# Order list with GpSimd's passes and the shared port, GpSimd's sums interleaved with the next products, VectorE's score blocks from the first period on

## The chip, the cores and the metric

The kernel runs on one core of one Trainium2 chip. A time is the device time of one execution in microseconds (us). The kernel before takes 893.42 us, the median of 3 runs (892.31 to 895.25).

A core has five engines, each with its own instruction queue that it works through in order: TensorE (PE, matrix products), VectorE (DVE), ScalarE (ACT, exponents), GpSimd (POOL) and SyncE (SP, which here issues all DMA transfers). Engines wait for each other on semaphores only.

## The reference

Two attention blocks over the same input x (2048 tokens, 512 features, 32 heads of 16 features), mixed by a gate for each token:

```python
def reference(A_x, A_wqkv, A_wo, B_x, B_wqkv, B_wo, gate_w):
    # _A_ref: full attention
    scores = jnp.einsum("bhqd,bhkd->bhqk", q, k) * (Dh ** -0.5)
    p = _softmax(scores, axis=-1)
    o = jnp.einsum("bhqk,bhkd->bhqd", p, v)
...
    # _B_ref: each token looks at 8 tokens: itself and 2, 4, ... 14 before it
    W, dil = 8, 2
    idx = pos[:, None] - off[None, :]
    logits = jnp.einsum("bhsd,bhswd->bhsw", q, kg) * scale
    attn = _softmax(logits, axis=-1)
    o = jnp.einsum("bhsw,bhswd->bhsd", attn, vg)
...
    x = A_x
    g = _sigmoid((x * gate_w).sum(-1, keepdims=True))
    a = _A_ref(x, A_wqkv, A_wo)
    b = _B_ref(x, B_wqkv, B_wo)
    return g * a + (1 - g) * b
```

Each block ends in a product with its own output matrix. All tensors are bfloat16.

## The kernel before

**Full attention (block A).** The work is cut into 32 *periods*: four chunks of 512 queries, and in each eight groups of four heads. A period has 64 *score blocks*, one for each of its four heads and each of 16 key tiles: 128 keys by 512 queries. For a score block TensorE multiplies keys and queries into PSUM; an exponent is taken; and TensorE multiplies the result with the values and adds it up in one PSUM bank (`acc`). The exponents go two ways:

- *On ScalarE*: score blocks are taken in sets of three and two (tile `ring`), with one ACTIVATE a set that writes `pT`. `pT` has five buffers.
- *On VectorE*: a block's scores go to a PSUM bank `D`; one TENSOR_SCALAR turns them into a 16-bit number (tile `dt_a`, or a part of `wkv` once the weights in it are used up), four such blocks side by side; then four passes over the 2048 columns (tile `pd_a`, again with spare parts) make four shifted approximations of the exponent. They are multiplied with four copies of the values that carry four weights (`vd_all`). `n_dve` says how many of a period's 64 blocks go this way: 0 in the first four periods, then 4, 8, 4, 8, then 8 and 12 in turn; 264 in all, so that ScalarE keeps 1784.

Between two periods VectorE moves `acc` out (`accT`, po1), divides by the sums (po2) and transposes (po3).

**Local attention (block B).** 16 tiles of 128 tokens (`b_tile`, line 776). For each: TensorE projects keys, values and queries, VectorE copies them out (`kvs`, `qb`), SyncE writes keys and values to a scratch in memory (`kv_scr`) and reads them back shifted by the eight offsets, in two halves of four offsets (`ksh` and `vsh`, two buffers each). GpSimd does the arithmetic, two offsets at a time:

- `logits_mul` (835): four products of 256 elements into `prod`, which has one buffer;
- `logits_add` (846): sums over the 16 features of a head by halving: two passes of 256 elements, one of 256, one of 128, and one of 64 into `lg`;
- softmax over the eight offsets: `sm_pre` on VectorE (max `mx` and subtraction), an exponent on ScalarE, `sm_post` on VectorE;
- `av_mul` (887) and `av_add` (904): four products of weights and values, then the sums into `ob` and at the end `obb`.

Then TensorE transposes `obb` (four transposes a tile, line 946 in `fin`), VectorE copies them to `obt`, and the output product (`ab_part`) adds both blocks for 128 tokens. Tile t+1's logits come ahead of tile t's weighted sums on GpSimd.

**What sets the order.** Every piece of work is an `Op` with an engine, a length that the author put in (`occ`), a due time (`dl`), what it needs (`deps`) and the buffers it takes and uses (`Tok`, `Res`). `list_schedule` (line 149) goes through time, starts on each engine the op with the earliest due time among those that can start, and returns all ops in the order of their planned starts. The instructions are then issued in that order on every engine and tied to it. So the lengths do not change the work; they decide where on each queue an instruction stands, and an engine that comes to an instruction whose input is late waits there with all that is behind it. Where the list sees TensorE idle it adds products with a zero tile (`z`) that keep it busy. GpSimd's work is entered as one op for four products (2.52 or 2.41 us) and one op for their sums (2.68, 1.37 or 2.74); when such an op meets one of VectorE's `pd_a` passes in the plan, both are stretched by fixed factors (`BESIDE`, `UNDER`). The due times of block B come from `b_start` and `b_space`: tile t is due `b_space` after tile t-1. The four scaled copies of the values (`evd`, line 669, in `v_proj`) are one op for each tile of keys, four TENSOR_SCALAR, entered with 0.43 + 0.032 us a head.

In the profile nearly all instructions of VectorE, ScalarE, GpSimd and SyncE have line 315 and those of TensorE line 324, where a helper records each one; so it is read by the names of the tiles. The line numbers given here are those of the kernel before.

Of the kernel before, what the change touches and what calls it, by code (L numbers as in the profile page):

```python
# [41 lines left out]
NPT = 5  # L42
LATE0 = 8
NDL = 3
SPREAD = (0.85, 0.9)
# [18 lines left out]
class Op:  # L64

    def __init__(self, eng, occ, fn, dl, deps=(), alloc=(), use=(), lat=None, rel=0.0, name="",
                 mode="f", js=(), full=0.0, fill=False, scores=None, after=(), ride=False):
        self.scores, self.ride = scores, ride
        self.eng, self.occ, self.fn, self.dl, self.rel, self.name = eng, occ, fn, dl, rel, name
        self.mode, self.js, self.full, self.fill, self.filled = mode, list(js), full, fill, 0  # L70
        self.after = [d for d in after if d is not None]
        self.deps, self.alloc = [d for d in deps if d is not None], list(alloc)
        if lat is None:
            lat = 0.0 if eng == "pe" else (occ(0.0) if callable(occ) else occ) + LAT[eng]
# [13 lines left out]
BESIDE, UNDER = 0.575, 0.52  # L88
# [3 lines left out]
P1D, SHD = -100.0, 2.0  # L92
# [56 lines left out]
def list_schedule(ops, zeros):  # L149
# [16 lines left out]
    def avail(o):  # L166
        t = o.ready
        for tk in o.alloc:
            r = tk.res
            n = len(r.order)  # L170
            if n >= r.cap:
                for u in r.order[n - r.cap].ops:
                    if u.done is None:
                        return INF
                    t = max(t, u.done)
# [15 lines left out]
    shift, glob = (0.0, 0.0), (0.0, 0.0)  # L191
    while len(out) < len(ops):
# [24 lines left out]
        if e == "pe":  # L217
            tz, n = arr.idle(o, t)
            if n > 0:
                z = zeros(n)  # L220
                tz = max([tz, avail(z)] + [u.t for tk in z.alloc[0].res.order[-2:] for u in tk.ops if u.done is not None and u.t < t])
                if tz + n * PASS + (0.0 if o.mode == "c" else SWITCH) <= t + 0.05:
# [3 lines left out]
                    z.done = end + LAT[e]  # L226
# [6 lines left out]
        else:  # L233
            occ, lat = o.occ, o.lat
            if e == "pool" and occ > 1.3:
                more = max(0.0, min(shift[1], t + occ / UNDER) - max(shift[0], t)) * (1.0 - UNDER)
                occ, lat, glob = occ + more, lat + more, (t, t + occ + more)
            if callable(occ):
                occ = o.occ(t)
                if glob[0] <= t < glob[1]:  # L240
                    occ /= BESIDE
                    free["pool"] += (min(t + occ, glob[1]) - t) * (1.0 - UNDER)
                lat = o.lat + occ
                shift = (t, t + occ)
            o.t, o.end, o.done = t, t + occ, t + max(occ, lat)
# [3 lines left out]
        for s_ in succ.get(o, ()):  # L249
            left[s_] -= 1  # L250
            if left[s_] == 0:
                s_.ready = max([s_.rel] + [d.end if d.eng == s_.eng else d.done for d in s_.deps] + [d.t for d in s_.after])
# [5 lines left out]
def kernel(  # L258
# [154 lines left out]
    rowc = const.tile([128, 3], FP32, name="rowc")  # L413
    z32 = const.tile([128, 32], BF16, name="z32")
# [24 lines left out]
    def init_dve():  # L439
# [8 lines left out]
        V.memset(z32[:], 0.0)  # L448

# [31 lines left out]
    def load_x(sc):  # L481
        def s():
            xl = work.tile([128, W // 2, D], BF16, name="xld", tag=("ksh", "vsh")[sc % 2], bufs=2)
# [31 lines left out]
    xtok = [tok(("ksh", "vsh")[sc % 2], 2) for sc in range(NC)]  # L515
    tw = tok("pd", NPD)
    o_x = [None] * NC
# [70 lines left out]
    def k_proj(i, sc, tag, dl, rel=0.0):  # L588
# [16 lines left out]
        return op("dve", 0.78, kc, dl, deps=[b], use=[tk])  # L605

    def k_bound(i, dl):
# [21 lines left out]
        a = op("dve", 0.3, mx, dl - 2.5, deps=o_kc[i])  # L629
        b = op("pe", 0.1, sw, dl - 2.0, full=0, deps=[a, o_perm], alloc=[tk])  # L630
        c = op("dve", 0.2, ng, dl - 1.2, deps=[b], use=[tk])
        if i == 0:
            o_k[i] = [op("dve", 0.32, fill(sc * QW, (sc + 1) * QW), dl + 0.1 * sc, deps=[c]) for sc in range(NC)]
        else:
            o_k[i] = [op("dve", 0.95, fill(0, S), dl, deps=[c])] * NC
# [14 lines left out]
    def v_proj(h0, h1, tb, TB, tag, dl, rel=0.0):  # L650
# [18 lines left out]
        def evd(t):  # L669
            def s():  # L670
                for m in range(NV):
                    V.tensor_scalar(out=vd_all[:, m, t - (NT - NTD), h0:h1, :], in0=vp_all[:, t, h0:h1, :],
                                    scalar1=WEIGHTS[m] * 2.0 ** -DEXP, scalar2=None, op0=ALU.mult)
            return s
# [7 lines left out]
        for t in range(max(tb, NT - NTD), tb + TB):  # L682
            d = op("dve", 0.43 + 0.032 * (h1 - h0), evd(t), max(dl, S0[4]) + 2.0, deps=[c])
            for h in range(h0, h1):
                o_vd[(h, t)] = d
# [12 lines left out]
    def q_proj(pi, tag, dl, rel=0.0):  # L698
# [25 lines left out]
        o_q[pi] = op("dve", 0.35, ab, dl, deps=[c], use=[tq])  # L724
# [51 lines left out]
    def b_tile(t):  # L776
# [45 lines left out]
        def load(key, off, hf):  # L822
            def s():
                r0 = 16 + t * 128 - DIL * hf * WH
                base = kv_scr[r0:r0 + 128, off * D:(off + 1) * D]
                st[key, hf] = work.tile([128, WH, D], BF16, name=key, tag=key, bufs=2)
                SP.dma_start(out=st[key, hf][:], in_=_ap(base, [[2 * D, 128], [-DIL * 2 * D, WH], [1, D]]))
            return s
        tks, tvs = [tok("ksh", 2), tok("ksh", 2)], [tok("vsh", 2), tok("vsh", 2)]
# [5 lines left out]
        def logits_mul(hf, wp):  # L835
            def s():
                if hf == 0 and wp == 0:
                    st["lg"] = work.tile([128, H, W], FP32, name="lg", tag="lg", bufs=2)
                st["prod"] = work.tile([128, WP, D], FP32, name="prod", tag="prod", bufs=1)
                for w_ in range(WP):  # L840
                    for c0 in range(0, D, HB):
                        G.tensor_tensor(out=st["prod"][:, w_, c0:c0 + HB], in0=st["ksh", hf][:, wp + w_, c0:c0 + HB],
                                        in1=st["qb"][:, c0:c0 + HB], op=ALU.mult)
            return s

        def logits_add(hf, wp):
            def s():
                lg = st["lg"]
                pv_ = st["prod"][:].rearrange("p w (h d) -> p w h d", d=DH)
                n = DH  # L850
                while n > 2:
                    n //= 2
                    ws = min(WP, max(1, HB // (H * n)))
                    for w0 in range(0, WP, ws):
                        G.tensor_tensor(out=pv_[:, w0:w0 + ws, :, 0:n], in0=pv_[:, w0:w0 + ws, :, 0:n],
                                        in1=pv_[:, w0:w0 + ws, :, n:2 * n], op=ALU.add)
# [6 lines left out]
            return s  # L863

        def sm_pre():
            lg = st["lg"]
            mx = work.tile([128, H], FP32, name="mx", tag="mx", bufs=1)
            V.tensor_reduce(out=mx[:], in_=lg[:], axis=AX.X, op=ALU.max)
            mx_bc = _ap(mx[:], [list(mx[:].ap[0]), [1, H], [0, W]])
# [5 lines left out]
        def sm_post():  # L875
# [4 lines left out]
            V.reciprocal(out=rr[:], in_=ssum[:])  # L880
            V.tensor_scalar(out=rr[:], in0=rr[:], scalar1=omg[:, t:t + 1], scalar2=None, op0=ALU.mult)
            rr_bc = _ap(rr[:], [list(rr[:].ap[0]), [1, H], [0, W]])
# [4 lines left out]
        def av_mul(hf, wp):  # L887
            def s():
                if wp == 0:
                    key = ("ob", "obb")[hf]  # L890
                    st[key] = work.tile([128, D], (FP32, BF16)[hf], name=key, tag=key, bufs=1)
                attn = st["lg"]
                st["prod"] = work.tile([128, WP, D], FP32, name="prod", tag="prod", bufs=1)
                for w_ in range(WP):
                    for c0 in range(0, D, HB):
                        w0 = hf * WH + wp + w_
                        a0 = attn[:, c0 // DH:c0 // DH + hn, w0:w0 + 1]
                        attn_bc = _ap(a0, [list(a0.ap[0]), [W, hn], [0, DH]])
                        G.tensor_tensor(out=st["prod"][:, w_, c0:c0 + HB].rearrange("p (h d) -> p h d", d=DH),
                                        in0=st["vsh", hf][:, wp + w_, c0:c0 + HB].rearrange("p (h d) -> p h d", d=DH),  # L900
                                        in1=attn_bc, op=ALU.mult)
            return s

        def av_add(hf, wp):
            def s():
                prod, ob = st["prod"], st["ob"]
                for c0 in range(0, D, HB):
                    cs = slice(c0, c0 + HB)
                    if not hf and not wp:
                        G.tensor_tensor(out=ob[:, cs], in0=prod[:, 0, cs], in1=prod[:, 1, cs], op=ALU.add)  # L910
                        continue
                    G.tensor_tensor(out=prod[:, 0, cs], in0=prod[:, 0, cs], in1=prod[:, 1, cs], op=ALU.add)
                    G.tensor_tensor(out=(st["obb"] if hf and wp else ob)[:, cs], in0=ob[:, cs], in1=prod[:, 0, cs], op=ALU.add)
            return s

        def chain_ops(fs, dls, deps, alloc, use, last_use=()):
            a = None
            for n_, (f, d, occ) in enumerate(fs):
                if n_ % 2 == 0:
                    tp = tok("prod", 1)  # L920
                a = op("pool", occ, f, dls + 0.01 * n_, deps=deps if a is None else [a],
                       alloc=(alloc if a is None else []) + ([] if n_ % 2 else [tp]),
                       use=use + (alloc if a is not None else []) + ([tp] if n_ % 2 else []), name=f"B{t}")
            return a
        lgs = [[(g(hf, wp), 0, c) for wp in range(0, WH, WP) for g, c in ((logits_mul, 2.52), (logits_add, 2.68))] for hf in range(2)]
# [358 lines left out]
```

## Time and profile before

| what | value |
|---|---|
| median of 3 runs | 893.42 us (892.31 to 895.25) |
| the profiled execution | 894.26 us |
| its span, first to last instruction | 892.1 us |
| mean clock granted to TensorE | 0.983 |
| exponents of block A on ScalarE | 714 ACTIVATE, 816.6 us |
| GpSimd's block-B passes | 1056, from 37.1 to 851.7 us |
| exponents of block A on VectorE | 264 passes `pd_a`, 963 and 960 ns; 264 passes from `D`, 681 and 682 ns |

The profile is of one execution. Each engine has its busy time; a group's row has its count, busy time and mean length, and the idle time just before its instructions with the engine that ended it. The page cuts the span into 40 slices with the busy share of each in tenths. The chain that ended last is followed back from the last instruction, each time to what released it; its shares say which engines' work set the end. An engine may have a high busy share and yet not set it, or wait seldom and set it all the same.

### The profile page before, as it was taken

What the parts mean: (1) busy time and instruction counts of PE and PEld (TensorE: products, weight loads), DVE (VectorE), ACT (ScalarE), POOL (GpSimd) and SP (SyncE); (2) the same over time, 40 slices, a digit from 0 to 9 for tenths busy, and PEclk for the clock granted to TensorE, in tenths of its full rate; (3) what the DMA queues carried; (4) which work ended last, traced back from release to release, by engine and by line L of the source; (5) the groups of instructions that cost most, each with busy time, mean ns of one, the idle gap of its engine ahead of it and who ended that gap; (6) DMA issues with size and microseconds to landing.
All of it is one profiled execution on the core that took longest, in us unless ns stands there. A gap on an engine that the chain in (4) does not pass through costs nothing.

```text
span 892.1 us, 18870 instructions
## 1 busy us (share of the span) xinstructions
PE 817.3 (92%) x7413; PEld 260.0 (29%) x7413; DVE 675.7 (76%) x1120; ACT 825.3 (93%) x736; POOL 786.4 (88%) x1088
## 2 busy tenths in 40 slices
PE   7898988987899999999999988999999999999997
PEld 3333323333232222222222222222223222222231
DVE  4344747688767988888797978888798787868866
ACT  2889999997999999999999998999999999999996
POOL 4369999999999999999999999999999999999910
PEclk9889999999999999999999999999999999999999
DMA  8310302020202111111112111011111210101000
GB/s 281 111 61 1 105 15 93 15 72 26 95 24 73 60 61 48 36 49 48 47 37 65 65 38 48 31 59 44 60 48 43 66 48 25 48 2 37 12 1 24
DMA packets 44440, 47.37 MB, mean 53 GB/s; under 512 B 2352, under 2 KB 41776, under 8 KB 44352
## 3 DMA queue, kind: packets, MB, share of 16 engines
q1 hardware_dynamic: 44352, 46.18, 16.0%
q8 instruction: 58, 0.95, 0.4%
q14 instruction: 30, 0.25, 0.1%
HBM read 39.85 MB, written 6.32 MB: 52 GB/s over the span
## 4 chain that ended last, share of the span: by engine, by line
POOL 51%; PE 16%; ACT 12%; DVE 11%; issue 8%; DMA 1%; POOLq 0%; SPq 0%; DVEq 0%; ACTq 0%
POOL prod L315 43%; ACT pT L315 12%; PE misc_ps L324 6%; PE ring L324 4%; PE acc L324 4%; POOL ob L315 4%; POOL obb L315 2%; DVE pd_a L315 2%; POOL lg L315 2%; DVE dt_a L315 1%; DVE wkv L315 1%; DVE lg L315 1%; PE D L324 1%; DVE vd_all L315 1%; DVE kt_all L315 1%
## 5 line engine op out<-in xcount | busy, mean ns | idle before, releaser
L315 ACT ACTIVATE pT<-ring 128x1536 bf16<-128x1536 f32 x714 | 816.6, 1301 | 41.2 <-PE acc L324 20.7
L324 PE MATMUL ring<-qt,kt_all 32*128 32x512 bf16 x1784 | 282.0, 386 | 29.6 <-ACT pT L315 24.3
L315 POOL TENSOR_TENSOR prod<-prod 128x256 f32<-128x256 f32 x352 | 278.9, 800 | 10.0
L315 POOL TENSOR_TENSOR prod<-ksh,qb 128x256 f32<-128x256 bf16 x256 | 184.9, 752 | 32.9 <-DMA ksh<-kv_scr 21.4
L324 PE MATMUL acc<-pT,vp_all 128*17 128x512 bf16 (+1 forms) x1784 | 194.1, 390 | 0.9 <-DVE accT L315 0.7
L315 POOL TENSOR_TENSOR prod<-vsh,lg 128x256 f32<-128x256 bf16 x256 | 182.1, 741 | 5.0
L324 PEld LDWEIGHTS <-kt_all 32*128 32x128 bf16 x2048 | 90.8, 91 | 300.8 <-issue 292.3
L324 PE MATMUL misc_ps<-z 128*32 128x512 bf16 x507 | 158.6, 385 | 2.6 <-DVE z L315 1.6
L315 DVE TENSOR_SCALAR pd_a<-wkv 128x2048 uint16<-128x2048 uint16 x160 | 150.1, 963 | 1.3
L315 DVE TENSOR_SCALAR wkv<-D 128x512 uint16<-128x512 f32 x160 | 109.0, 681 | 43.3 <-PE D L324 42.7
L324 PE MATMUL acc<-pd_a,vd_all 128*17 128x512 bf16 x1056 | 108.3, 385 | 3.9 <-DVE pd_a L315 3.0
L324 PE MATMUL D<-qt,kt_all 32*128 32x512 bf16 x264 | 100.9, 382 | 6.6 <-DVE dt_a L315 2.9
L315 DVE TENSOR_SCALAR pd_a<-dt_a 128x2048 uint16<-128x2048 uint16 x104 | 97.2, 960 | 0.8
L315 DVE TENSOR_SCALAR dt_a<-D 128x512 uint16<-128x512 f32 x104 | 70.9, 682 | 34.7 <-PE D L324 33.8
L324 PEld LDWEIGHTS <-z 128*32 128x32 bf16 x621 | 54.5, 96 | 76.1 <-issue 45.7
L324 PEld LDWEIGHTS <-vp_all 128*17 128x17 bf16 (+1 forms) x1784 | 44.7, 88 | 84.7 <-issue 78.1
L324 PE MATMUL misc_ps<-bw,xT 128*128 128x512 bf16 x192 | 56.3, 390 | 7.5 <-DVE qt L315 3.6
L315 POOL TENSOR_TENSOR ob<-ob,prod 128x256 f32<-128x256 f32 x64 | 56.1, 877 | 5.0
L315 DVE TENSOR_SCALAR_CACHE_REDUCE kt_all<-misc_ps,rowc 128x512 bf16<-128x512 f32 x32 | 23.9, 748 | 30.7 <-PE misc_ps L324 30.6
L324 PEld LDWEIGHTS <-vd_all 128*17 128x17 bf16 x1056 | 30.7, 88 | 50.3 <-issue 42.2
L324 PEld LDWEIGHTS <-xT 128*128 128x128 bf16 x576 | 30.5, 98 | 42.5 <-issue 37.0
L324 PE MATMUL misc_ps<-xT,wkv 128*32 128x512 bf16 x384 | 38.4, 389 | 3.7 <-DVE xT L315 1.9
(78 smaller groups left out, 607.5 us busy)
## 6 DMA issues: line engine op xcount, KB each, us to landing
ksh<-kv_scr SPq DMA_DIRECT2D x32, 512.0 KB, 4.0
vsh<-kv_scr SPq DMA_DIRECT2D x32, 512.0 KB, 3.7
kv_scr<-kvs SPq DMA_DIRECT2D x16, 256.0 KB, 2.0
xld<-in_A_x_dram SPq DMA_DIRECT2D x4, 512.0 KB, 6.8
out_dram<-osb SPq DMA_DIRECT2D x16, 128.0 KB, 1.7
bw<-in_B_wqkv_dram SPq DMA_DIRECT2D x1, 1536.0 KB, 10.1
wkv<-in_A_wqkv_dram SPq DMA_DIRECT2D x2, 512.0 KB, 6.9
pd_a<-in_A_wqkv_dram SPq DMA_DIRECT2D x1, 512.0 KB, 8.0
```

Source lines behind the costliest of these rows:

```text
L315: return chain_on(key, f(*a, **k))
L324: return chain(nc.tensor.matmul(out, lhsT=lhsT, rhs=rhs, start=start, stop=stop, **kw))
```

## The change

It has these parts:

1. *The list's costs.* GpSimd's work is entered pass by pass, each as 0.14 us of its own (`PRE`) and then a time per element (`NS`) in which it holds a port shared with VectorE. VectorE's 16-bit passes (`SB`) and its passes with two inputs of 64 elements or more (`TT`) hold the same port. In the plan only one holds it at a time. An op that needs another op of the same engine may start `SELF` behind its end (0.11 us on GpSimd). Several lengths are changed to match.
2. *GpSimd's order within a tile.* `prod` has two buffers. The sums of one pair of offsets are issued in turn with the products of the next pair. In the weighted sums the two halves of each step are issued next to each other.
3. *Scaled values.* `vd_all` is made by one TENSOR_TENSOR with a small tile of weights (`wts`) for a block of heads instead of four TENSOR_SCALAR for each key tile: 5 instructions instead of 60, due from the first period on.
4. *VectorE's blocks*: 4 in each of the first four periods, 8 in each of the next four, then 8, 8, 8, 12 in turn. The sum is still 264.
5. *Buffers*: keys, values and the first three loads of x share one tag `gat` with three buffers, and the key and value loads are tied to one order on SyncE's queue (keys of tile t+1, then values of tile t). `pT` becomes three buffers of three blocks and three of two.
6. *Due times*: `b_start` 36, `b_space` 44, 47 and 49; accT's eviction ahead of everything on VectorE; an output tile needs only its own tile's `obt`, not those of its whole chunk.

The core of the diff:

```diff
-    n_dve=(0,) * 4 + (4, 8) * 2 + (8, 12) * 12,
+    n_dve=(4,) * 4 + (8,) * 4 + (8, 8, 8, 12) * 6,
...
-    b_start=40.0,
-    b_space=(41.0,) * 4 + (44.5,) * 4 + (47.5,) * 8,
+    b_start=36.0,
+    b_space=(44.0,) * 4 + (47.0,) * 4 + (49.0,) * 8,
...
-NPT = 5
+NPT = 3
+NGA = 3
...
-SPREAD = (0.85, 0.9)
+SPREAD = (0.75, 0.8)
...
+SELF = dict(pe=0.0, dve=0.09, act=0.05, pool=0.11, sp=0.0)
+NS = dict(bb=0.00189, bf=0.00178, ff=0.00212)
+PRE = 0.14
+SB = lambda n: [(True, 0.065 + n / 3840.0)]
+TT = lambda n: [(n >= 64, 0.075 + n / 960.0)]
...
-            occ, lat = o.occ, o.lat
-            if e == "pool" and occ > 1.3:
...
+            occ = o.occ
+            if o.parts is not None:
+                u = t
+                for shared, p in o.parts:
+                    if shared:
+                        u = port = max(u, port) + p
+                    else:
+                        u += p
+                occ = u - t
...
-        def evd(t):
-            def s():
-                for m in range(NV):
-                    V.tensor_scalar(out=vd_all[:, m, t - (NT - NTD), h0:h1, :], in0=vp_all[:, t, h0:h1, :],
-                                    scalar1=WEIGHTS[m] * 2.0 ** -DEXP, scalar2=None, op0=ALU.mult)
...
+        def evd():
+            w = wts[:]
+            k0, n_ = t0 - (NT - NTD), (h1 - h0) * (DH + 1)
+            V.tensor_tensor(out=vd_all[:, :, k0:k0 + nt, h0:h1, :].rearrange("p m t h d -> p m t (h d)"),
+                            in0=_ap(vp_all[:, t0, h0, 0:1], [list(vp_all[:].ap[0]), [0, NV], [H * (DH + 1), nt], [1, n_]]),
+                            in1=_ap(w, [list(w.ap[0]), [1, NV], [0, nt], [0, n_]]), op=ALU.mult)
...
+        lseq = lgs[0][:nm]
+        for g_ in range(len(halves)):
+            nxt = lgs[g_ + 1][:nm] if g_ + 1 < len(halves) else []
+            ad = lgs[g_][nm:]
+            lseq += ad[:2]
+            for k_ in range(max(nm, na - 2)):
+                lseq += nxt[k_:k_ + 1] + ad[2 + k_:3 + k_]
...
+    turn = loads["k", 0]
+    for t in range(NT):
+        turn = turn + loads.get(("k", t + 1), []) + loads["v", t]
+    for o1, o2 in zip(turn, turn[1:]):
+        o2.after.append(o1)
...
-        a = op("dve", 0.64, po1, E - 1.0, deps=o_pv[pi], alloc=[ta], use=[acc_tok[pi]])
+        a = op("dve", 0.64, po1, E - PO1D, deps=o_pv[pi], alloc=[ta], use=[acc_tok[pi]])
...
-                   deps=[a] if k0 else [o_oat[NG * c_ + ng - 1], o_wo] + o_obt[TPC * c_:TPC * (c_ + 1)],
+                   deps=[a] if k0 else [o_oat[NG * c_ + ng - 1], o_wo] + o_obt[t:t + 1],
```

Here `lgs[g_]` holds the passes of one pair of offsets: `nm` = 4 products and `na` = 5 sums. So between two sums of one pair a product of the next pair is issued.

In the built programs VectorE issues the same 264 blocks, GpSimd the same passes in another order, and TensorE 443 + 120 products with the zero tile instead of 507 + 114.

More of the change, by code (lines that the diff above doesn't have):

```diff
@@ L66, in __init__ @@
     def __init__(self, eng, occ, fn, dl, deps=(), alloc=(), use=(), lat=None, rel=0.0, name="",
-                 mode="f", js=(), full=0.0, fill=False, scores=None, after=(), ride=False):
-        self.scores, self.ride = scores, ride
+                 mode="f", js=(), full=0.0, fill=False, scores=None, after=(), ride=False, parts=None):
+        self.scores, self.ride, self.parts = scores, ride, parts
+        if parts is not None:
+            occ = sum(p for _, p in parts)
         self.eng, self.occ, self.fn, self.dl, self.rel, self.name = eng, occ, fn, dl, rel, name
@@ L87 @@
 SH_LAT = 0.3
-BESIDE, UNDER = 0.575, 0.52
 GT = 32.0
@@ L174, in avail @@
                         return INF
-                    t = max(t, u.done)
+                    t = max(t, u.end + SELF[u.eng] if u.eng == o.eng else u.done)
         return t
@@ L225, in list_schedule @@
                     z.t, end = arr.put(z, tz)
-                    z.done = end + LAT[e]
+                    z.end, z.done = end, end + LAT[e]
                     extra.append(z)
@@ L251, in list_schedule @@
             if left[s_] == 0:
-                s_.ready = max([s_.rel] + [d.end if d.eng == s_.eng else d.done for d in s_.deps] + [d.t for d in s_.after])
+                s_.ready = max([s_.rel] + [d.end + SELF[d.eng] if d.eng == s_.eng else d.done for d in s_.deps] + [d.t for d in s_.after])
                 cand[s_.eng].append(s_)
@@ L448, in init_dve @@
         V.memset(z32[:], 0.0)
+        for m in range(NV):
+            V.memset(wts[:, m:m + 1], WEIGHTS[m] * 2.0 ** -DEXP)
     def init_pool():
@@ L885, in b_tile, with av_mul @@
         hn = HB // DH
-        def av_mul(hf, wp):
+        def av_mul(hf, wp, w_, c0):
             def s():
-                if wp == 0:
+                if wp == 0 and w_ == 0 and c0 == 0:
                     key = ("ob", "obb")[hf]
                     st[key] = work.tile([128, D], (FP32, BF16)[hf], name=key, tag=key, bufs=1)
+                if w_ == 0 and c0 == 0:
+                    st["prod", hf, wp] = work.tile([128, WP, D], FP32, name="prod", tag="prod", bufs=2)
                 attn = st["lg"]
[L893 to L902, printed above, removed]
@@ L904, in av_add @@
-        def av_add(hf, wp):
-            def s():
[L906 to L911, printed above, removed]
+                w0 = hf * WH + wp + w_
+                a0 = attn[:, c0 // DH:c0 // DH + hn, w0:w0 + 1]
+                attn_bc = _ap(a0, [list(a0.ap[0]), [W, hn], [0, DH]])
@@ new lines, in s, with av_add @@
+                G.tensor_tensor(out=st["prod", hf, wp][:, w_, c0:c0 + HB].rearrange("p (h d) -> p h d", d=DH),
+                                in0=st["vsh", hf][:, wp + w_, c0:c0 + HB].rearrange("p (h d) -> p h d", d=DH),
+                                in1=attn_bc, op=ALU.mult)
+            return s, "bf", HB
+        def av_add(hf, wp, c0, k_):
+            def s():
+                prod, ob = st["prod", hf, wp], st["ob"]
+                cs = slice(c0, c0 + HB)
+                if not hf and not wp:
+                    G.tensor_tensor(out=ob[:, cs], in0=prod[:, 0, cs], in1=prod[:, 1, cs], op=ALU.add)
+                elif k_ == 0:
@@ new lines, in chain_ops @@
+        def chain_ops(seq, dls, alloc, toks):
+            made, tps, a, seen = {}, {}, None, set()
+            for n_, (g_, k_, (f, kind, n), src, deps) in enumerate(seq):
+                new = g_ not in tps
+                if new:
+                    tps[g_] = tok("prod", 2)
+                al, us = list(alloc.get((g_, k_), ())), []
+                for tk_ in toks(g_):
+                    if tk_ not in al:
+                        us.append(tk_)
+                (al if new else us).append(tps[g_])
+                a = op("pool", 0.0, f, dls + 0.001 * n_, deps=deps + ([made[g_, src]] if src is not None else []),
+                       after=[a], alloc=al, use=us, name=f"B{t}", parts=[(False, PRE), (True, NS[kind] * n)])
+                made[g_, k_] = a
+            return a
@@ new lines, in b_tile @@
+        halves = [(hf, wp) for hf in range(2) for wp in range(0, WH, WP)]
+        mulp = lambda g, hf, wp: [g(hf, wp, w_, c0) for w_ in range(WP) for c0 in range(0, D, HB)]
+        adds = []
+        n_ = DH
+        while n_ > 2:
+            n_ //= 2
+            ws = min(WP, max(1, HB // (H * n_)))
+            adds += [(n_, w0, ws) for w0 in range(0, WP, ws)]
+        nm, na = WP * (D // HB), len(adds) + 1
+        lgs = []
+        for g_, (hf, wp) in enumerate(halves):
+            ps_ = mulp(logits_mul, hf, wp) + [logits_add(hf, wp, *x) for x in adds] + [logits_out(hf, wp)]
+            srcs = [None] * nm + [1, 3] + list(range(nm + 1, nm + na - 1))
+            lgs.append([(g_, k_, p_, srcs[k_], ([lk[hf], qa] if k_ == 0 else [])) for k_, p_ in enumerate(ps_)])
@@ new lines, in b_tile @@
+        a = op("dve", 0.0, sm_gate, tb + SMD, deps=[a, o_g], parts=[(True, 0.1)])
+        a = op("dve", 0.0, sm_mul, tb + SMD, deps=[a], use=[tlg], parts=TT(H * W))
+        for g_, (hf, wp) in enumerate(halves):
+            k1 = range(1 if not hf and not wp else 2)
+            ps_ = mulp(av_mul, hf, wp) + [av_add(hf, wp, c0, k_) for k_ in k1 for c0 in range(0, D, HB)]
+            srcs = [None] * nm + [2, 3] + [nm, nm + 1]
+            aseq += [(g_, k_, p_, srcs[k_], ([lv[hf], a] if k_ == 0 else [])) for k_, p_ in enumerate(ps_)]
```

136 lines of the change are left out of this document (66 added, 70 removed).

## The prediction

> **What bounds the kernel now.** I read the page's busy shares first, then the chain that ended last, then the table of windows, the waits and short pieces of the timeline. Shares and chain, from the page:
>
> ```profile
> PE 817.3 (92%) x7413; PEld 260.0 (29%) x7413; DVE 675.7 (76%) x1120; ACT 825.3 (93%) x736; POOL 786.4 (88%) x1088
> ...
> ACT  2889999997999999999999998999999999999996
> POOL 4369999999999999999999999999999999999910
> ...
> POOL 51%; PE 16%; ACT 12%; DVE 11%; issue 8%; DMA 1%; POOLq 0%; SPq 0%; DVEq 0%; ACTq 0%
> ```
>
> ScalarE (ACT) is the fullest engine, yet half of the chain that ended last is GpSimd (POOL). GpSimd is busy without a break from about 75 us to 850 us. The windows show what that does to ScalarE (columns: window, then busy us and count of PE, PEld, DVE, ACT, POOL, then TensorE's clock):
>
> ```profile
> 25.00:50.00 25.00, 23.24 (x233) 8.19 (x232) 6.94 (x26) 20.68 (x20) 12.25 (x21) 0.80 0.31 96
> 50.00:75.00 25.00, 23.41 (x289) 8.91 (x285) 13.40 (x41) 24.78 (x24) 17.35 (x29) 1.00 0.17 54
> ...
> 200.00:225.00 25.00, 20.27 (x192) 8.37 (x188) 21.13 (x39) 18.84 (x17) 23.82 (x37) 0.93 0.08 23
> ...
> 525.00:550.00 25.00, 21.28 (x175) 5.71 (x175) 18.13 (x27) 22.30 (x21) 23.90 (x35) 0.93 0.17 54
> ...
> 700.00:725.00 25.00, 22.27 (x206) 6.23 (x199) 22.40 (x33) 22.81 (x21) 24.21 (x30) 1.00 0.15 46
> ```
>
> Summed over the whole table, ScalarE stands idle 2.7 us of 150 between 50 and 200 us (1.8%), and 30.9 us of 650 between 200 and 850 us (4.8%). How GpSimd, which feeds ScalarE nothing but one small exponent a tile, can stop it shows in the waits (engine waiting, what it waited for: total us, times, longest) and in the timeline around 802 us (start, duration, engine):
>
> ```profile
> ACT pT L315 <- PE acc L324: 20.7, 16, 5.0
> ...
> PEld L946 <- POOL obb L315: 9.0, 8, 2.0
> DVE mx L315 <- POOL lg L315: 7.5, 7, 2.5
> ...
> PE misc_ps L946 <- POOL obb L315: 7.0, 5, 1.8
> ```
> ```profile
> 802.04 0.31 POOL L315 TENSOR_TENSOR lg<-prod 128x64 f32<-128x64 f32 x1
> 802.38 0.42 DVE L315 TENSOR_REDUCE mx<-lg 128x32 f32<-128x256 f32 x1 [1.49 <-POOL lg L315]
> ```
>
> TensorE and VectorE work through fixed orders. The order list puts a tile's four transposes (L946) and its softmax (mx) where it believes GpSimd will be done. In the trace, the transposes of tiles 0 to 4 start 2.6 to 4.5 us after GpSimd's obb is written, those of tiles 6 to 15 mostly 0.1 to 1.0 us after it; mx starts 0.03 us after lg in seven of the last eight tiles. So from about 400 us on GpSimd is later than the list thinks, TensorE and VectorE stand at these instructions, and all score blocks queued behind them come late. GpSimd's steady pace is (802.4 - 436.6)/7 = 52.3 us a tile between the softmaxes of tiles 8 and 15.
>
> I count score blocks (one ring matmul each, 1784 in all) in front of a tile's transposes in the built instruction order, and set them against the trace: tile 4 has 585 in front and starts at 307.3 us, tile 6 808 at 409.8, tile 8 1020 at 512.5, tile 14 1668 at 825.3, tile 15 1723 at 851.8. Pace: 0.460 us a block from tile 4 to 6, 0.483 from 8 to 14; from tile 0 (190 at 114.5) to 1 (285 at 159.1) 0.469. ScalarE's own floor is 816.6/1784 = 0.458.
>
> **The change part by part.**
>
> *GpSimd's dependent passes.* Four passes of a weighted sum, before:
>
> ```profile
> 102.94 0.73 POOL L315 TENSOR_TENSOR prod<-prod 128x256 f32<-128x256 f32 x1
> 103.75 0.72 POOL L315 TENSOR_TENSOR ob<-ob,prod 128x256 f32<-128x256 f32 x1
> 104.43 0.72 POOL L315 TENSOR_TENSOR prod<-prod 128x256 f32<-128x256 f32 x1
> 105.23 0.73 POOL L315 TENSOR_TENSOR ob<-ob,prod 128x256 f32<-128x256 f32 x1
> ```
>
> Start to start it is 0.81 and 0.80 us where a pass needs the one just before, 0.68 where it does not: 0.12 us a dependence. By the code a tile has 26 such neighbours (16 in the logits, where prod has one buffer, so the next product waits too; 10 in the weighted sums); the trace has 414 such gaps for 16 tiles. Interleaved and with two prod buffers, three a tile stay (the sums of the last pair of offsets). 23 x 0.12 = 2.8 us a tile, 44 us in all: 49.5 instead of 52.3 a tile. The other bound is nothing, if VectorE's hold on the port fills what the gaps leave. I take most of it, since a gap of 0.12 us is short beside a VectorE pass of 0.68 us or more.
>
> The Trainium skill (SBUF — State Buffer, section "SBUF: two separate sides") says that GpSimd and VectorE share a port pair as an exclusive lock for the whole instruction, for VectorE passes in a two-port mode or with two SBUF inputs. The trace agrees in that the pd_a pass takes 0.675 us at the least and 1.05 at the median, and a 256-element GpSimd pass 0.72 or about 1.17. By that rule a gap taken out is partly a gap in which VectorE got in anyway, and the saving is less than 44; its result is the second rival below.
>
> *The order list.* In the built order of the changed kernel the transposes have 203, 305, 405, 520, 625, 735 ... 1605, 1715, 1765 blocks in front (before 190, 285, 388, 480, 585, 698 ... 1560, 1668, 1723), about 110 a tile. At 0.465 us a block that is 51.2 us a tile: GpSimd at 49.5 keeps ahead. Behind tile 15's transposes 19 blocks are left instead of 61. This takes away the two L946 waits (16.0 us) and mx (7.5 us), and with them most of what held ScalarE after 200 us. Next late is ScalarE itself.
>
> *The scaled values vd_all.* Sixty TENSOR_SCALAR (13.1 + 2.3 = 15.4 us in the groups) become five TENSOR_TENSOR, two of 816 elements and three of 1632. No such pass is in the trace. From rden (16 elements, 0.18 us at 211.3 us) and lg<-lg,mx (256, 0.42 at the least) I get 1.0 ns an element: 1.0 and 1.8 us, together 7.4; at ott's mean of 646 ns for 256 elements 16.5. I take 7.4, since the uncontended row is the nearer in kind. The worth is in the place: the largest stall of the whole run is
>
> ```profile
> 205.83 2.54 DVE L315 TENSOR_SCALAR vd_all<-vp_all 128x136 bf16<-128x136 bf16 x4
> ...
> 211.54 1.02 ACT L315 ACTIVATE pT<-ring 128x1024 bf16<-128x1024 f32 x1 [5.01 <-PE acc L324]
> ```
>
> where four passes, which the old list costs at 0.69 us together, take 2.54 and make accT and the next period late. It goes, 5 us.
>
> *VectorE's blocks from the first period.* The count stays: 264 blocks, 1784 exponents' blocks. Each costs VectorE 0.68 + 0.96 = 1.65 us. The first four periods get 4 each (6.6 us in some 28, where windows show 7 to 16 of 25 busy), the next four 8 instead of 4 and 8, the late ones 9 on average instead of 10. ScalarE's sum is unchanged, so by itself this is worth 0; it evens VectorE out (22 to 23.7 of 25 in windows like 650 to 675 now). Without that cover, periods 4 to 7 are the tight ones: see the last rival.
>
> *Buffers and queue.* Three gather buffers for keys and values instead of four, loads in a forced order on SP's queue: a half tile lasts GpSimd some 12 us, and a load lands 3.4 to 6.2 us after its issue, two halves ahead; 0, and up to 1.5 us a tile (24) if loads queue behind a late store there. Six exponent buffers instead of five and accT's eviction first: these act on "ACT pT <- PE acc", 20.7 us; between 0 and that, counted within the pace below.
>
> **The sum.** Up to block 285 (159.1 us) I change nothing. The other 1499 blocks at 0.465 (between the 0.460 and 0.469 of the stretches where GpSimd did not yet press) take 697.0: 856.1. Now the 61 blocks after tile 15's transposes end with the span after 40.3 us, of which 61 x 0.483 = 29.4 is pace and 10.9 tail. 856.1 + 10.9 = 867.0 of span. The profiled execution took 894.26 for 892.1 of span (+2.2) and stands 0.8 above the median: 868.4, **869** said.
>
> **The rivals.**
> 1. *ScalarE without a stall*: pace 0.458 from block 285 on. Speaks for it that windows of 24.9 and 25.0 busy exist; against, that no long stretch keeps it. 686.5 instead of 697.0: 858.
> 2. *GpSimd binds as before* because the port eats the gaps: its end stays at 851.7, and 19 blocks at 0.483 plus 10.9 follow: 871.8 of span, 873. It decides if less than 1.1 of the 2.8 us a tile survives.
> 3. *The list is no truer than before*, stalls come back elsewhere, for each one removed: 893. For it: the chain also has PE, DVE and ACT pieces (490 to 514, 594 to 669 us); against: the misjudged costs are just those named above.
> 4. *Slower: VectorE becomes the bound in periods 1 to 7*, where projections, scaled values and the new blocks meet. Busy is 21 of 25 from 200 to 250 us now; 4 more blocks add 6.6. If each of the seven periods lost what the window 200 to 225 loses (6.2 us, 5.7 over the usual), that is 40: 909. It decides from 3.5 us a period on, where the gain is used up. Against: VectorE stood at 7 to 16 of 25 in periods 0 to 3, and 8 us of vd_all go.
>
> **How the numbers follow.** Forecast 0.58 (869), rival 1 0.12, rival 2 0.15, rival 3 0.06, rival 4 0.09. A measurement of this kernel tells about 0.3% (2.7 us) from no change: faster 0.85, same 0.06, slower 0.09. The range holds the forecast and rivals 1 and 2 (0.85): its low end is rival 1 less the 4.3 us that ScalarE loses in the window 25 to 50 us, should the first blocks on VectorE relieve it there, 854; its high end is rival 2 with half of the 24 us that queued loads could cost, 885.
>
> **What would show it.** Right: GpSimd at 49 to 50 us a tile, gaps between its passes nearly gone; the L946 waits on obb and mx on lg down from 23.5 us to a few; ScalarE idle about 2% of 200 to 850; the 5 us stall gone; the chain led by ACT or PE. Wrong: mx or the transposes still starting at once behind GpSimd (rival 2), VectorE above 24 of 25 before 260 us with "ACT pT <- PE acc" grown (rival 4), or key and value loads that GpSimd waits for.

## The result, and the profile after

The changed kernel takes 879.12 us (median of 4 runs, 878.21 to 882.45), the kernel before on the same chip 893.76: ratio 0.9843, interval 0.9812 to 0.9874. The forecast was 869; of the 24 us it promised, 14.6 came. From the page of the changed kernel (span 880.7 us):

```profile
PE 793.0 (90%) x7310; PEld 257.8 (29%) x7355; DVE 694.6 (79%) x1069; ACT 820.7 (93%) x736; POOL 781.6 (89%) x1088
...
ACT  2889996589899999999999999999999999999996
POOL 5287999379999999999999999999999999999830
...
ACT 43%; PE 22%; issue 18%; DVE 15%; DMA 1%; SPq 0%; DVEq 0%; ACTq 0%
```

GpSimd, 51% of the chain before, is no longer in it at all; ScalarE leads. But both rows have a hole in the seventh to ninth of the 40 slices that was not there before. The windows:

```profile
125.00:150.00 25.00, 16.00 (x160) 5.34 (x158) 19.76 (x20) 16.22 (x15) 24.77 (x40) 0.80 0.07 22
150.00:175.00 25.00, 14.57 (x143) 6.26 (x144) 21.48 (x24) 15.19 (x15) 11.27 (x18) 0.80 0.18 60
...
200.00:225.00 25.00, 23.32 (x263) 8.53 (x266) 23.29 (x45) 23.44 (x22) 24.77 (x35) 1.00 0.16 54
...
525.00:550.00 25.00, 23.99 (x207) 7.65 (x207) 17.47 (x26) 25.00 (x23) 24.76 (x38) 1.00 0.07 22
...
700.00:725.00 25.00, 22.69 (x194) 6.99 (x197) 20.95 (x31) 24.96 (x24) 25.00 (x34) 1.00 0.36 105
```

From 200 to 850 us ScalarE is idle 5.0 us of 650 (30.9 before): better than forecast. From 50 to 200 us it is idle 22.9 of 150 (2.7 before), 18.6 of it in the first two windows shown, where TensorE's granted clock also falls to 0.80. The waits say who was waited for there:

```profile
POOL prod L320 <- DVE qb L320: 27.9, 2, 20.0
...
ACT pT L320 <- PE ring L329: 16.9, 10, 8.6
...
PE acc L329 <- DVE pd_a L320: 11.4, 12, 8.3
ACT pT L320 <- PE D L329: 10.6, 2, 9.5
PE misc_ps L329 <- DVE vp_all L320: 10.3, 5, 9.1
```

ScalarE waits for TensorE, TensorE once for VectorE's `pd_a` (8.3 us) and once for its `vp_all` (9.1 us), and later GpSimd for VectorE's `qb`. VectorE's timeline has two instructions out of all proportion (start, duration); the second, `rden`, stands ahead of that `vp_all` in VectorE's queue:

```profile
127.08 0.68 DVE L320 CAST qt<-misc_ps 128x512 bf16<-128x512 f32 x1
127.68 8.93 DVE L320 TENSOR_SCALAR pd_a<-dt_a 128x2048 uint16<-128x2048 uint16 x1
136.52 0.21 DVE L320 SCALAR_TENSOR_TENSOR negk<-misc_ps,rowc 128x1 f32<-128x1 f32 x1
...
152.06 9.25 DVE L320 TENSOR_TENSOR rden<-rden,g_rw 128x16 f32<-128x16 f32 x1
161.34 0.42 DVE L320 TENSOR_TENSOR ott<-accT,rden 128x256 bf16<-128x256 f32 x1
```

The same pd_a pass takes 0.68 us when nothing is in its way, and `rden` has sixteen elements. In both stretches GpSimd runs pass after pass:

```profile
127.90 0.68 POOL L320 TENSOR_TENSOR prod<-ksh,qb 128x256 f32<-128x256 bf16 x1
128.53 0.73 POOL L320 TENSOR_TENSOR prod<-prod 128x256 f32<-128x256 f32 x1
129.20 0.68 POOL L320 TENSOR_TENSOR prod<-ksh,qb 128x256 f32<-128x256 bf16 x1
129.83 0.41 POOL L320 TENSOR_TENSOR prod<-prod 128x128 f32<-128x128 f32 x1
```

Each starts about 0.05 us before the one ahead ends. ScalarE, in the same stretch, with its two stalls:

```profile
138.76 16.43 ACT L320 ACTIVATE pT<-ring 128x1536 bf16<-128x1536 f32 x14 [8.59 <-PE ring L329]
164.71 1.45 ACT L320 ACTIVATE pT<-ring 128x1536 bf16<-128x1536 f32 x1 [9.52 <-PE D L329]
```

So a theory was at hand. **Theory 1 (port):** the interleaving took away the gaps by which VectorE gets the shared port; in two places it got none for 8 to 9 us. **Theory 2 (VectorE's load),** the fourth rival of the prediction: VectorE is overfull in these periods, since its blocks now start early.

### The profile page after: what moved, and what is told of

Its sections match the earlier page's. It is cut to its first block, busy times and chain, and to the rows that moved or that the text cites. A ratio compares the mean times of both kernels' runs of the same rounds, so it can differ in the third digit from the quotient of the medians.

```text
span 880.7 us, 18629 instructions
## 1 busy us (share of the span) xinstructions
PE 793.0 (90%) x7310; PEld 257.8 (29%) x7355; DVE 694.6 (79%) x1069; ACT 820.7 (93%) x736; POOL 781.6 (89%) x1088
## 3 DMA queue, kind: packets, MB, share of 16 engines
q1 hardware_dynamic: 44352, 46.18, 16.7%
## 4 chain that ended last, share of the span: by engine, by line
ACT 43%; PE 22%; issue 18%; DVE 15%; DMA 1%; SPq 0%; DVEq 0%; ACTq 0%
ACT pT L320 42%; PE misc_ps L329 8%; PE ring L329 7%; PE acc L329 6%; DVE pd_a L320 5%; DVE dt_a L320 2%; DVE rden L320 2%; DVE wkv L320 1%; PE D L329 1%; DVE kt_all L320 1%; DVE qt L320 1%; DMA xld<-in_A_x_dram 1%; DVE lg L320 1%; ACT lg L320 1%; DVE ott L320 1%
## 5 line engine op out<-in xcount | busy, mean ns | idle before, releaser
L320 POOL TENSOR_TENSOR prod<-prod 128x256 f32<-128x256 f32 x352 | 272.2, 786 | 2.5
L320 POOL TENSOR_TENSOR prod<-ksh,qb 128x256 f32<-128x256 bf16 x256 | 198.2, 782 | 51.2 <-DVE qb L320 27.9
L320 POOL TENSOR_TENSOR prod<-vsh,lg 128x256 f32<-128x256 bf16 x256 | 189.2, 770 | 3.5 <-DVE lg L320 3.5
L320 DVE TENSOR_SCALAR pd_a<-wkv 128x2048 uint16<-128x2048 uint16 x144 | 140.9, 1015 | 3.3 <-PE acc L329 2.4
L320 DVE TENSOR_SCALAR wkv<-D 128x512 uint16<-128x512 f32 x144 | 98.3, 683 | 51.2 <-PE D L329 50.7
L329 PE MATMUL misc_ps<-z 128*32 128x512 bf16 x443 | 136.9, 385 | 1.9 <-DVE z L320 1.6
L320 DVE TENSOR_SCALAR pd_a<-dt_a 128x2048 uint16<-128x2048 uint16 x120 | 123.8, 1058 | 0.4
L320 DVE TENSOR_SCALAR dt_a<-D 128x512 uint16<-128x512 f32 x120 | 81.7, 681 | 39.4 <-PE D L329 37.8
L329 PEld LDWEIGHTS <-z 128*32 128x32 bf16 x563 | 48.0, 96 | 62.5 <-issue 34.3
L329 PE MATMUL acc<-z 128*32 128x512 bf16 x120 | 39.1, 386 | 0.0
```

The source lines that it names most:

```text
L320: return chain_on(key, f(*a, **k))
L329: return chain(nc.tensor.matmul(out, lhsT=lhsT, rhs=rhs, start=start, stop=stop, **kw))
```

## The experiments

**The dependences back** (`e1_deps_back`): the changed kernel, its list and all, with GpSimd's sums one after the other.

```diff
-            lseq += ad[:2]
-            for k_ in range(max(nm, na - 2)):
-                lseq += nxt[k_:k_ + 1] + ad[2 + k_:3 + k_]
+            lseq += ad + nxt
...
-            ps_ = mulp(av_mul, hf, wp) + [av_add(hf, wp, c0, k_) for k_ in k1 for c0 in range(0, D, HB)]
+            ps_ = mulp(av_mul, hf, wp) + [av_add(hf, wp, c0, k_) for c0 in range(0, D, HB) for k_ in k1]
...
```

> The changed kernel with GpSimd's sums issued one after the other again (each needs the one before; 18 dependent neighbours a tile instead of 3), all else kept, the list included. Theory 1 (port): the two stalls of ScalarE at 130 and 155 us in the changed kernel (8.6 and 9.5 us) come from two VectorE passes that waited 8.3 and 9.1 us for the port, because GpSimd's stream has no gap any more in which VectorE gets in. Then no VectorE pass here waits longer than one GpSimd pass (none over 1.3 us), both stalls are gone, and GpSimd is slower by 15 x 0.12 = 1.8 us a tile, some 29 us in all, which its present idle of 33 us and its lead of 15 to 20 us can take: 862 to 875 us. Theory 2 (VectorE's load): VectorE is overfull between 125 and 230 us since its blocks start early; then stalls of 5 us and more stay there and the time is 880 or above.

Measured: 868.68 us, ratio to before 0.9723 (0.9707 to 0.974). Both stalls are gone. The five `vd_all` passes apart, no VectorE pass is over 1.4 us; two of `kt_all`, at 1.37 and 1.32, just miss the 1.3 expected. GpSimd takes 50.0 us a tile (49.2 in the changed kernel, from the ends of `obb` of tiles 10 to 14), 0.8 more instead of the 1.8 expected, and is still off the chain. Undoing the part of the change that was to make GpSimd faster makes the kernel 10 us faster.

**One gap a group** (`e2_one_gap`): interleaved as in the change, but one pass in eight or nine needs the one before.

```diff
-            lseq += ad[:2]
-            for k_ in range(max(nm, na - 2)):
-                lseq += nxt[k_:k_ + 1] + ad[2 + k_:3 + k_]
+            lseq += ad[:3]
+            for k_ in range(nm):
+                lseq += nxt[k_:k_ + 1] + ad[3 + k_:4 + k_]
...
-            ps_ = mulp(av_mul, hf, wp) + [av_add(hf, wp, c0, k_) for k_ in k1 for c0 in range(0, D, HB)]
+            ps_ = mulp(av_mul, hf, wp) + [av_add(hf, wp, c0, k_) for k_ in k1 for c0 in (HB, 0)]
...
```

> The changed kernel with one dependent neighbour in each group of eight or nine GpSimd passes (the third sum follows the second at once; in the weighted sums the first sum follows the last product), 8 a tile more than now, 0.9 us a tile. Theory 1 (port): a lost turn at the port ends at the next gap, so no VectorE pass waits over 5.2 us and most likely none over 1.3; the two stalls go and with them TensorE's lower clock there: 858 to 866 us, faster than both kernels. Theory 2 (VectorE's load): the stalls at 125 to 200 us stay: 878 to 884.

Measured: **865.35 us**, ratio 0.9693 (0.9678 to 0.9707), the fastest of all. The trace has ten dependences a tile, and `vd_all` apart no VectorE pass over 1.3 us. The windows of the two stalls in this kernel:

```profile
125.00:150.00 25.00, 22.76 (x239) 9.11 (x242) 20.30 (x33) 24.90 (x24) 24.45 (x35) 1.00 0.12 38
150.00:175.00 25.00, 23.03 (x258) 7.69 (x261) 23.44 (x41) 22.96 (x21) 24.77 (x34) 1.00 0.18 60
```

VectorE does the same early blocks here, is busier than in the changed kernel (23.44 of 25), and ScalarE is fed: theory 2 falls. This kernel and the changed one are 13.8 us apart. The list plans each of these kernels anew, so how much of that is the lost turns alone is not separated; the kernels that test the port by itself, below, have no list.

**The old count of blocks, without gaps** (`e3_blocks_before`): `n_dve=(0,) * 4 + (4, 8) * 2 + (8, 12) * 12` in the changed kernel.

> The changed kernel with the count of VectorE's blocks of the kernel before (0 in the first four periods, then 4, 8, 4, 8, then 8 and 12 in turn). Theory 2 (VectorE's load): no stall over 3 us between 125 and 200 us, and 862 to 870 in all. Theory 1 (port): whether a pass loses its turn is a matter of when it asks, so the stalls fall elsewhere or not at all; one or more VectorE passes over 1.3 us may still be seen anywhere, as GpSimd's stream has no gaps; and the periods with 12 blocks make ScalarE idle more late in the run: 865 to 885.

Measured: four executions of 896.89, 921.42, 931.77 and 933.51 us, too far apart for a ratio with an interval; the profile is of the first. Both expectations missed the time: theory 2 wanted 862 to 870, theory 1 865 to 885. The stalls fall elsewhere, as theory 1 allows: from VectorE's timeline in this run

```profile
43.91 8.90 DVE L320 TENSOR_SCALAR d<-e 128x16 f32<-128x16 f32 x1 [4.92 <-ACT e L320]
```

a pass of sixteen elements waits 8.6 us, and `kt_all` at 226 us takes 7.48. No profile of the other three executions was taken, so what made them longer still is open.

**The port by itself** (`m1_port`, `m2_port_quiet`, `m3_port_threshold`): kernels that compute nothing of the reference, with GpSimd's passes and VectorE's requests alone.

> Not the computation: it leaves all of it out and writes zeros. Three stretches, each with 180 GpSimd passes of 256 elements and 80 VectorE passes of 2048 uint16 elements like pd_a, a copy from PSUM of changing length before each so that they ask at changing times. In the first no GpSimd pass needs the one before, in the second every ninth does, in the third every second. Theory 1 (port): in the first stretch at least one VectorE pass waits over 2 us, in the second none over 6 us, in the third none over 1.3 us. Theory 2: VectorE never waits for more than one GpSimd pass in any stretch (1.3 us at most).

Measured: none of 240 VectorE passes over 1.3 us, in any stretch. A miss for theory 1: a stream without gaps is not enough. VectorE asked about every second pass here. Back in the traces, I counted for each VectorE pass that needs the port how many GpSimd passes had run just before it without a gap and without giving way. In the changed kernel, some 400 requests after fewer than 10 such passes wait at most 0.56 us (but for one of 1.7 us that followed a lost turn at once); the long waits of the changed kernel and of `e3_blocks_before` stand behind 12 or more. In the kernel before no request stands behind more than 5. So theory 1 became one of run length:

```diff
-NREQ = 80
-EVERY = (0, 9, 2)
+STRETCH = ((40, (13, 23)), (40, (5, 9)), (9, (13, 23)))
...
```

> Not the computation: it leaves all of it out and writes zeros. Three stretches of 280 GpSimd passes of 256 elements. In the first, a pass that needs the one before comes every 40 passes, and VectorE asks for the port only after 13 to 22 copies from PSUM (some 11 to 20 GpSimd passes); in the second the same, but after 5 to 8 copies (4 to 8 passes); in the third VectorE asks as rarely as in the first, but every ninth GpSimd pass needs the one before. Theory 1a (run length): VectorE loses its turn when GpSimd has run about 12 passes without a gap and without giving way. Then in the first stretch several VectorE passes take over 2 us, the wait ending at GpSimd's next gap at the latest; in the second and third none is over 1.3 us. Theory 1b (mere chance of the moment of asking): lost turns in the first stretch no more often than in the second, none or one in all.

Measured: in the first stretch six of eleven requests take 4.7 to 16.7 us, each ending in GpSimd's next dependent pass; in the second none of 34, in the third none of 14 is over 1.3. So it is not mere chance of the moment (theory 1b). From the timeline of the first stretch:

```profile
23.77 0.72 POOL L32 TENSOR_TENSOR prod<-fa 128x256 f32<-128x256 f32 x1
24.40 6.49 DVE L32 TENSOR_SCALAR pd<-dt 128x2048 uint16<-128x2048 uint16 x1
24.45 0.66 POOL L32 TENSOR_TENSOR prod<-ka,qa 128x256 f32<-128x256 bf16 x1
...
29.68 0.66 POOL L32 TENSOR_TENSOR prod<-ka,qa 128x256 f32<-128x256 bf16 x1
30.41 1.05 POOL L32 TENSOR_TENSOR prod<-prod,fa 128x256 f32<-128x256 f32 x1
```

VectorE asks at 24.4 and gets in at 30.2, in the gap ahead of the pass at 30.41 that needs the one before. By count, requests after 10, 11, 11, 12 and 13 undisturbed passes won, those after 14, 15, 16, 16, 17 and 18 lost.

> Not the computation: it leaves all of it out and writes zeros. Three stretches of 280 GpSimd passes of 256 elements, each with a pass that needs the one before every 30. In the first, VectorE is quiet for 9 to 16 copies (some 8 to 14 GpSimd passes) before each 2048-element pass; in the second for 16 to 21 copies (14 to 19 passes), but every ninth GpSimd pass has 64 elements only and needs nothing; in the third as long, and VectorE asks with a two-input pass of 16 elements (like rden). Theory 1a (run length, as the stretch before this showed it: 11 lost in none, 14 and more in all): in the first the requests after 12 passes or fewer win, those after 14 lose; in the third nearly all requests lose, whatever their size; in the second they lose too, if only a dependence or a lost turn makes an opening, and win if a short pass is one.

Measured: in the first stretch all 19 requests won, behind 0 to 13 passes. In the second all nine (14 to 19) lost, waiting 5.9 to 8.8 us each, to the next dependence: a short pass was no opening here. In the third seven of eleven waited 7.2 to 8.8 us, all behind 16 or more; one behind 13 and one behind 14 won, and so did two that came at the dependent pass itself. So a pass of 16 elements loses its turn as one of 2048 does.

**What the other parts are worth**, each undone in the kernel with one gap a group (865.35). These three ran on another chip, where the kernel before takes 893.30 instead of 892.89. *The old count of blocks* (`e4_gap_blocks_before`):

> The kernel with one gap a group and the old count of VectorE's blocks (0 in the first four periods, then 4, 8, 4, 8, then 8 and 12). What the blocks from the first period on are worth by themselves. Theory 1 (port): the 897 to 934 us of the run without gaps came from lost turns at the port alone, so with gaps no VectorE pass is over 1.3 us (vd_all apart) and the time is back at 866 to 876, a few us above the one with early blocks, since periods with 12 blocks press VectorE. Rival: the old count does not fit the new list in itself (the 12-block periods make ScalarE idle): 885 and more.

Measured: 870.36, ratio 0.9726 (0.9688 to 0.9764); no long VectorE pass. With gaps the old count costs 5.0 us (2.9 by the two ratios, whose intervals overlap, so this is not clear of noise); without gaps it cost 17.8 at the least, over the changed kernel. GpSimd's pace goes from 49.5 to 51.0 us a tile with the old count, which has more VectorE blocks in the late periods.

*The scaled values by sixty passes* (`e5_gap_scaled_before`):

```diff
-            d = op("dve", 0.0, evd, dl + 2.0, deps=[c], parts=TT(NV * nt * (h1 - h0) * (DH + 1)))
...
+            d = op("dve", 0.43 + 0.032 * (h1 - h0), evd(t), dl + 2.0, deps=[c])
```

> The kernel with one gap a group and the sixty TENSOR_SCALAR for the scaled values instead of five TENSOR_TENSOR, entered in the list with their old lengths, but due as early as now. If the sixty short passes were what cost 5 us at 206 us in the kernel before, they make VectorE late by about 2 us at each of the blocks of eight heads here too: 867 to 873. If the five long passes, which hold the port 1.8 us each, cost as much: 862 to 866, no slower.

Measured: 880.82, ratio 0.9838 (0.9794 to 0.9882): 15.5 us slower (13.0 by the two ratios), more than either expectation. The sixty passes take 24.0 us, where the changed kernel's five take 7.9. ScalarE has done its first 400 blocks at 233.7 us, against 218.4 with one gap a group, so the whole loss falls there. The list still enters four of these passes at 0.69 us, while at 216 us in this trace they take 2.16: the 15.5 us hold both the passes and their untrue length, and these were not separated.

*A list that does not know the port is shared* (`e6_gap_list_no_port`); the work is the same, only its order differs:

```diff
-                        u = port = max(u, port) + p
+                        u += p
```

> The kernel with one gap a group and a list that knows each pass but not that the port is shared (GpSimd and VectorE may hold it at once in the plan); the work is the same. Theory of the prediction (a list that believes GpSimd early makes TensorE and VectorE stand at transposes and softmax): planned GpSimd is some 8 us a tile too fast, the softmax starts at once behind GpSimd in most tiles and the waits of L1001 on obb come back: 880 to 895. Rival: the true gain is in blocks, buffers and scaled values, and the list's port does not matter: 864 to 870.

Measured: 948.91, ratio 1.0605 (1.0557 to 1.0652), worse than expected and worse than the kernel before. Its waits:

```profile
PEld L1001 <- POOL obb L320: 25.9, 11, 4.5
DVE mx L320 <- POOL lg L320: 25.6, 9, 6.1
...
PE misc_ps L1001 <- POOL obb L320: 22.2, 11, 4.2
```

and the chain that ended last, from its page:

```profile
POOL 43%; PE 20%; DVE 15%; ACT 13%; issue 8%; DMA 1%; SPq 0%; DVEq 0%; POOLq 0%; ACTq 0%
```

GpSimd, which the chain of the changed kernel does not hold, has 43% of it again. The waits are the prediction's three, 73.7 us instead of 23.5: most transposes start 0.06 us behind `obb`, most softmaxes 0.03 us behind `lg`. In the changed kernel they start 7 to 22 us behind from tile 2 on. This is not the old list, which knew the port by fixed factors: the old list with the other parts of the change was not run. Nor were the buffers and the due times undone (parts 5 and 6).

## Why the prediction was right or wrong

- **What bounds the kernel: right.** GpSimd held TensorE and VectorE at transposes and softmax through a list that believed it early. e6 shows the mechanism: with the port taken out of the list, for GpSimd and VectorE alike, those waits return, GpSimd is back in the chain with 43%, and the time rises by 83.6 us.
- **GpSimd's dependent passes: the pace came out, in part by luck, and what it was to bring did not.** 414 gaps became 48, three a tile, and the pace is 49.2 us a tile (forecast 49.5). But the price of 0.12 us a gap does not hold beside VectorE's passes: with 15 dependences a tile back (e1) the pace is 50.0, 0.8 us more and not 1.8. In tiles 10 to 14 GpSimd has no idle time in either kernel but these gaps; the gaps cost e1 its 1.8 us, and its 66 passes take 1.1 us less in sum. Part of the 3.1 us a tile that GpSimd gained on the kernel before is the smaller count of VectorE's late blocks instead, which by e4 makes 1.5 us a tile. And with a true list GpSimd is off the path: e1 is faster by 10 us.
- **The step that failed** is the other bound of that term: "nothing, if VectorE's hold on the port fills what the gaps leave". It let the missing gaps cost GpSimd at most its saving, and VectorE nothing. In the runs GpSimd kept 0.8 of the 1.8 us for 15 gaps, and VectorE lost its turn: twice for 8.3 and 9.1 us over its own length, and once, at 348 us, for 2.0, each time after a long undisturbed run of GpSimd's. The two long ones are 18.1 us of ScalarE's time; e2, where VectorE loses no turn, is 13.8 us faster. The Trainium skill (SBUF — State Buffer, "SBUF: two separate sides") says that whichever starts first holds the port pair for its whole instruction and the other blocks. By that a wait should end with one instruction. Most here do, at 0.6 us or less, but the longest VectorE pass in m2 took 16.65 us, 0.68 of it its own, and waited through more than twenty GpSimd passes.
- **The order list: right, and too low.** The L946 waits on `obb`, 16.0 us, are gone (the line is now L1001; a row of 2.3 us on `prod` is left, 2.2 before), and mx waits no more. The pace behind block 400 is (833.2 - 238.2)/1300 = 0.458 us a block (starts of the 401st and the 1701st ring product), the first rival's floor, where 0.465 was forecast: 1384 blocks x 0.007 = 10 us better. Up to block 400 it is some 25 us later than the forecast's 212.6, the 18.1 us of the lost turns among them. The two together make the miss of 13.7 us of span in the profiled execution, 10 in the median. That the time came out in the stated range, 854 to 885, is to that extent luck: a loss and a gain that the forecast did not have offset each other.
- **Scaled values: direction right, size too small.** 5 us was read from one stall; undone in the kernel with one gap a group, with their old lengths in the list, they cost 15.5. The five passes took 998 ns at the least and 1849 at the median (1.0 and 1.8 forecast).
- **Blocks from the first period: priced 0**; 5.0 us by e4, not clear of noise.
- **Rivals.** The first came true after 240 us. The second, GpSimd binding, did not come, though its premise, that the port eats gaps, did in part. The third, a list no truer than before, did not come: its waits are gone. The fourth had the right place and the wrong cause: VectorE was late in those periods, but kept from the port, not overfull (at most 23.3 of 25 us in any window up to 250 us). The three single parts, 83.6, 15.5 and 5.0, are each measured with the rest in place and do not add up to the gain.

## What to carry to other kernels

When an order is written ahead, the truth of its costs can be worth more than the speed of an engine: here 84 us hung on one line of the list, and the 1.6% by which fewer dependences quickened GpSimd (50.0 to 49.2 us a tile) was worth less than nothing. Before removing the small gaps in one engine's stream, ask who else uses them: here one dependent pass in eight or nine, at 0.12 us or less, was opening enough. An instruction many times longer than its own minimum is the first thing to look for in a trace; group means hide it (pd_a's mean rose from 0.96 to 1.03 us).

## What the runs showed of the hardware

GpSimd and VectorE normally take turns at the port pass by pass: in the kernel before VectorE waits out one pass (at most some 0.6 us). In m2 and m3, after 14 or more GpSimd passes back to back, with no dependence between neighbours and no turn given, VectorE's request was left waiting in 22 of 23 cases until GpSimd met a dependence (passes of up to 16.65 us; two that came at the dependence itself are not counted). The count of 14 is for passes of 256 elements. In the full kernels it is less sharp: of the requests behind 12 or 13 passes some were lost and some won. The wait for `rden` in the changed kernel ended when GpSimd ran out of work at 161.3 us.

The list counts a VectorE pass with two inputs as a holder of the port only from 64 elements on (`TT`), and enters `rden`, of sixteen, without it. The runs show otherwise: `rden` waited 9.1 us in the changed kernel, and a pass like it up to 8.8 us in m3.

Not settled: what in GpSimd makes the turn fail after some 14 passes; and why the first long wait in the changed kernel, at 136 us, and the one in `e3_blocks_before`, at 52.8 us, ended beside a pass of 64 elements with no gap ahead of it, while 64-element passes made no opening in m3.
